# Soft-MoE logits with slots on partitions, one sum of weights per half, and side products placed anew

## The chip, the cores and the metric

The kernel runs on one core of a Trainium2 chip. The metric is the device time of one execution in microseconds (us); less is better. The kernel before takes 743.97 us (median of 3 runs, 743.84 to 745.63). Engines are named as the profile names them: PE is the matrix engine and PEld its weight loads, DVE the vector engine, ACT the scalar engine, POOL the GpSimd engine, SP the engine that issues the DMAs.

## The reference, cut to what matters

Attention over 4 batches of 8 heads (1152 keys, 64 wide, queries pooled in twos to 576) gives x. A soft mixture of experts with 32 slots takes x, and a gated layer follows.

```python
attn = exp(scores - max);  attn = attn / (sum(attn) + 1e-09);  x = attn @ v      # [2304, 512]
logits = x @ phi                                                                 # [2304, 32]
d = softmax(logits, over tokens);  slot_input = d.T @ x                          # [32, 512]
slot_out[e] = relu(slot_input[e] @ w1[e]) @ w2[e]                                # 8 experts
c = softmax(logits, over slots);  x = c @ slot_out
xn = x / rms(x) * rms_g
out = (silu(xn @ w_gate) * (xn @ w_val)) @ w_out
```

## The kernel before

The attention works through 16 pairs of heads, p = 0 to 15, four pairs to a batch. Within a pair the two heads are s = 0, 1; queries lie in two halves h of 288, keys in nine tiles kt of 128. For each (kt, h) `qk` makes scores on PE (line 407, both heads side by side in the array), ACT makes exponentials `e` (L409), POOL adds them up in `acc` (L424), and PE multiplies them with v (`av`, L430). `acc` comes in two parts j for each half: tiles 0 to 4 and 5 to 8. In pairs 0 and 15 the halves come one after the other, and DVE makes part of the sums.

Work is written out by hand in program order, and every engine runs its own instructions in that order. A tile kt is a step; every third (kt = 2, 5, 8) is a visit, in which PE runs, after the scores, three items of the row maximum of a later pair (m1, m2, m3, L350 or L356, each reduced on DVE, L351 or L357, 128 x 1024 numbers) and the products `av` of three tiles (called a, b, c). The table `AT` puts side work at a time in units of kt: 2.75 is late in the first visit, ahead of b, 2.88 ahead of c. `side(p)` collects for pair p the side work of the pair before, l = p - 1: `take_x` copies av out of PSUM (L440), `sums` (2.75) adds the rows of `acc` over the 128 keys with a matmul against ones (L450: two heads, two halves, two parts, each 32 columns wide, so four can stand side by side in the array), `recips` (2.87) turns the sums so that tokens lie on partitions (L459) and takes their reciprocals, `x_logits` (5.78) multiplies x with phi, tokens on partitions (L500), `x_share` and `logit_add` divide and add up over heads (L509, L519, L520), `x_turn` and `x_divide` (8.75) put the finished x with tokens on partitions (L482, L491). At batch ends come `d_turn` and `d_exp` (8.73, 8.85: logits with slots on partitions, L537, and their exponentials, L557, with the add of their sums, L559), `d_back` (2.88, L565), `slot_part` (5.76, L580), `slot_turn` (8.74, L603) and the softmax over slots, `c_soft` (3.5, 5.53, 8.96; L611 to L624). Other side work on DVE: `low_q` (3.2, L308), `low_k` (L314), `turn_64` (0.5, 1.0, 3.3; L714), all with two inputs in SBUF. The two `max_tail` items (L360, L363) stand at 2.85 and 2.86.

All scores, maximum items and side products of PE take their PSUM from one tag of three buffers, in turn:

```python
def two_banks(name):
    return ps.tile([128, 2, 512], F32, tag="u", bufs=3, name=name)
```

so the third tile after a given one takes its buffer, and PE waits until that one has been read. After pair 15 the experts (L975, L998) and the gated layer (L1158, L1206) follow; the weights of the experts come in by DMA as the buffers of the attention come free.

Of the kernel before, what the change touches and what calls it, by code (L numbers as in the profile page):

```python
# [7 lines left out]
F32 = mybir.dt.float32  # L8
# [6 lines left out]
ALU = mybir.AluOpType  # L15
# [46 lines left out]
    x_share=5.785,  # L62
    logit_add=5.79,
# [10 lines left out]
    c_soft=[3.5, 5.53, 8.96],  # L74
# [20 lines left out]
)  # L95
AT_15 = dict(
    take_x=0.24,
    sums=0.8,
    recips=1.33,
    x_turn=[2.3, 3.3],  # L100
    x_divide=[2.4, 3.6],
    x_logits=4.2,
    x_share=4.8,
    drop_x=4.25,
    logit_add=5.22,
# [6 lines left out]
    logit_add_a=6.51,  # L112
# [37 lines left out]
def attention_softmoe_gated_kernel(ctx: ExitStack, tc: tile.TileContext, kT, qT, vv, ip, cst, w1, w2, wg, wv, wo, rg, out):  # L150
# [103 lines left out]
    ipt = one.tile([128, 4, 64], F32, name="ipt")  # L254
    rgt = one.tile([128, 4], F32, name="rgt")
# [185 lines left out]

    def sums(p, hs=(0, 1)):

        n = len(hs)
        o = bank([64 * n, HQ], "sums")
        for j in range(2):
            for s in (1, 0):
                for i, h in reversed(list(enumerate(hs))):
                    g = 32 * (n * s + i)
                    pe.matmul(o[g:g + 32, :], lhsT=ones, rhs=acc[p, h, j][:, s], start=(j == 0), stop=(j == 1))  # L450
        rel("B", 2 * n)
        srow[p] = B([64 * n, HQ], F32, "srow")
        ac.copy(srow[p], o)

    def recips(p, hs=(0, 1)):
        n = len(hs)
        o = bank([TB, 3, 64 * n], "sumt")
        for t in range(3):
            pe.transpose(out=o[:, t, :], in_=srow[p][:, TB * t:TB * t + TB], identity=ident[0:64 * n, 0:64 * n])  # L459
        rel("B")  # L460
        if p not in rr:
            rr[p] = S([TB, 2, 3, 2], "rr")
        r = rr[p][:, hs[0]:hs[-1] + 1]
        dv.tensor_scalar_add(out=r.rearrange("p h t s -> p s h t"),
                             in0=o.rearrange("p t (s h x) -> p s h t x", s=2, h=n)[:, :, :, :, 0], scalar1=1e-9)
        dv.reciprocal(r, r)

    xo, ls = {}, {}
# [59 lines left out]
    def d_turn(g):  # L528
# [80 lines left out]
    def c_max(b):  # L609
        mx = S([TB, NBK], "cmx")  # L610
        dv.reduce_max(out=mx, in_=lg[b], axis=AX.X)  # L611
        t = ct[b] = S([TB, NBK, 32], "ct", bufs=1)
        dv.tensor_tensor(out=t, in0=lg[b], in1=mx[:, :, None].to_broadcast([TB, NBK, 32]), op=ALU.subtract)
# [109 lines left out]
    def side(p):  # L723
# [3 lines left out]
        def at(name, g):  # L727
            ts = (AT_0 if p == 0 else AT_15 if p == NP - 1 else AT).get(name, AT.get(name))
# [22 lines left out]
        if l >= 0:  # L751
            at("take_x", lambda i: take_x(l))
            at("sums", lambda i: sums(l))
# [4 lines left out]
            at("x_logits", lambda i: x_logits(l, range(6)))  # L758
            at("x_share", lambda i: x_share(l, range(6)))
# [25 lines left out]
        if p == NP - 1:  # L785
# [5 lines left out]
            at("x_logits_a", lambda i: (x_logits(p, range(3)), x_share(p, range(3))))  # L791
            at("logit_add_a", lambda i: logit_add(p, (0,)))
# [7 lines left out]
    with tc.manual_schedule():  # L800
# [45 lines left out]
        dv.tensor_copy(identr, ident[0:TB, 0:TB])  # L846

# [455 lines left out]
```

## Time and profile before

| | |
|---|---|
| median of 3 runs | 743.97 us |
| the profiled execution | 744.83 us, of which the span of the page is 742.8 us |
| PE | busy 710.6 us, 96% of the span |
| DVE, ACT, POOL | busy 426.6, 391.7 and 423.3 us |
| pair 8 of the attention | 249.0 to 278.3 us |

The page gives busy times by engine, the span in 40 slices, the DMA queues, the chain of waits that ended last, and the costliest groups of instructions. One fp32 matmul of the program appears as two records (two passes), a transpose as one. A row's busy time merges instructions that follow closely; the start of the next row on the same engine tells when the array was free.

### The profile page before, as it was taken

What the parts mean: (1) busy time and instruction counts of PE and PEld (TensorE: products, weight loads), DVE (VectorE), ACT (ScalarE), POOL (GpSimd) and SP (SyncE); (2) the same over time, 40 slices, a digit from 0 to 9 for tenths busy, and PEclk for the clock granted to TensorE, in tenths of its full rate; (3) what the DMA queues carried; (4) which work ended last, traced back from release to release, by engine and by line L of the source; (5) the groups of instructions that cost most, each with busy time, mean ns of one, the idle gap of its engine ahead of it and who ended that gap; (6) DMA issues with size and microseconds to landing.
All of it is one profiled execution on the core that took longest, in us unless ns stands there. A gap on an engine that the chain in (4) does not pass through costs nothing.

```text
span 742.8 us, 15502 instructions
## 1 busy us (share of the span) xinstructions
PE 710.6 (96%) x6143; PEld 500.3 (67%) x6143; DVE 426.6 (57%) x663; ACT 391.7 (53%) x809; POOL 423.3 (57%) x340
## 2 busy tenths in 40 slices
PE   4999999999999999999999999979999999999998
PEld 2666677675676676676676665544357888888887
DVE  5958666676687675677765763351053755544420
ACT  2455665664665656656655534432155856554320
POOL 5336887866877876678876665320016854535330
PEclk9999999999999999999999999989999999999999
DMA  5222552753635635517514316079991010000001
GB/s 173 96 90 77 184 192 73 254 183 126 237 124 202 238 103 179 206 61 254 182 44 181 129 48 230 6 276 357 374 384 52 15 43 30 29 28 15 29 28 43
DMA packets 52855, 103.57 MB, mean 139 GB/s; under 512 B 5816, under 2 KB 19632, under 8 KB 52784
## 3 DMA queue, kind: packets, MB, share of 16 engines
q1 hardware_dynamic: 52784, 102.59, 39.3%
q8 instruction: 48, 0.79, 0.4%
q14 instruction: 23, 0.19, 0.1%
HBM read 89.39 MB, written 13.11 MB: 138 GB/s over the span
## 4 chain that ended last, share of the span: by engine, by line
PE 88%; DVE 5%; DMA 3%; issue 2%; ACT 1%; POOL 1%; SPq 0%; ACTq 0%; DVEq 0%
PE sc L407 21%; PE av L430 20%; PE yo L1206 20%; PE mxp L350 5%; PE gv L1158 3%; PE sums L450 2%; PE xl L500 2%; PE hin L975 2%; DVE mx L351 2%; PE xo L482 1%; PE so L998 1%; DMA w<-away 1%; PE mxp L360 1%; PE pp L580 1%; DMA w<-in_w_dram 1%
## 5 line engine op out<-in xcount | busy, mean ns | idle before, releaser
L424 POOL TENSOR_TENSOR acc<-acc,e 128x576 f32<-128x576 f32 x148 | 213.9, 1475 | 63.4 <-ACT e L409 57.9
L409 ACT ACTIVATE e<-sc 128x576 f32<-128x576 f32 x288 | 165.7, 658 | 95.4 <-PE sc L407 93.6
L351 DVE TENSOR_REDUCE mx<-mxp 128x2 f32<-128x1024 f32 x120 | 144.3, 1223 | 110.2 <-PE mxp L350 110.1
L430 PE MATMUL av<-e,vt 128*64 128x288 f32 x1152 | 164.7, 416 | 0.0
L424 POOL TENSOR_TENSOR acc<-e 128x576 f32<-128x576 f32 x60 | 84.7, 1432 | 89.6 <-ACT e L409 89.6
L430 PEld LDWEIGHTS av<-e,vt 128*64 128x64 f32 x1152 | 72.6, 136 | 60.1 <-issue 24.1
L1206 PE MATMUL yo<-woh,hA 128*128 128x512 f32 (+1 forms) x312 | 98.9, 384 | 0.0
L407 PE MATMUL sc<-qh,kh 64*128 64x288 f32 x576 | 96.7, 327 | 0.8 <-DVE mx L351 0.6
L407 PE MATMUL sc<-mr,pick 64*128 64x288 f32 x576 | 87.7, 295 | 1.5 <-DMA mr<-mrow 1.5
L407 PE MATMUL sc<-ql,kh 64*128 64x288 f32 x576 | 87.2, 294 | 0.0
L407 PE MATMUL sc<-qh,kl 64*128 64x288 f32 x576 | 87.1, 294 | 0.0
L1163 DVE SCALAR_TENSOR_TENSOR th<-th,gv 128x384 f32<-128x384 f32 x72 | 39.9, 554 | 62.4 <-ACT th L1160 61.8
L1189 POOL TENSOR_TENSOR hA<-hu,hA 128x384 fp32r<-128x384 f32 x48 | 48.9, 1019 | 42.5 <-ACT hA L1188 38.8
L407 PEld LDWEIGHTS sc<-qh,kh 64*128 64x128 f32 x576 | 55.5, 186 | 24.2 <-issue 9.8
L1206 PEld LDWEIGHTS yo<-woh,hA 128*128 128x128 f32 x312 | 57.6, 188 | 10.2 <-issue 0.7
L407 PEld LDWEIGHTS sc<-mr,pick 64*128 64x128 f32 x576 | 56.5, 187 | 1.9 <-DMA mr<-mrow 1.9
L1206 PE MATMUL yo<-wol,hA 128*128 128x512 f32 (+1 forms) x151 | 57.8, 383 | 0.0
L1160 ACT ACTIVATE th<-gv 128x384 f32<-128x384 f32 x72 | 35.2, 490 | 42.4 <-PE gv L1158 38.9
L407 PEld LDWEIGHTS sc<-qh,kl 64*128 64x128 f32 x576 | 56.6, 189 | 0.2
L407 PEld LDWEIGHTS sc<-ql,kh 64*128 64x128 f32 x576 | 56.2, 187 | 0.0
L350 PE MATMUL mxp<-kh,qh 64*128 64x512 f32 x240 | 48.6, 435 | 0.0
L1165 DVE SCALAR_TENSOR_TENSOR hu<-th,gv 128x384 f32<-128x384 f32 x72 | 39.9, 554 | 8.4 <-DVE th L1163 0.5
(192 smaller groups left out, 1040.4 us busy)
## 6 DMA issues: line engine op xcount, KB each, us to landing
w<-in_w_dram SPq DMA_DIRECT2D x86, 256.0 KB
w<-in_w_dram SPq DMA_DIRECT2D x21, 512.0 KB
vt<-in_vv_dram SPq DMA_DIRECT2D x16, 576.0 KB
qraw<-in_qT_dram SPq DMA_DIRECT2D x15, 576.0 KB
kraw<-in_kT_dram SPq DMA_DIRECT2D x15, 576.0 KB
away<-w SPq DMA_DIRECT2D x32, 256.0 KB
w<-away SPq DMA_DIRECT2D x32, 256.0 KB
raw<-in_wg_dram SPq DMA_DIRECT2D x12, 512.0 KB
```

What stands on the lines that cost most here:

```text
L350: pe.matmul(o[:, s, :], lhsT=q[r, 128 * t:128 * t + 128], rhs=k[r, 512 * c:512 * c + 512], start=True, stop=True)
L351: dv.reduce_max(out=heads[:, :, t, c], in_=o, axis=AX.X)
L407: pe.matmul(o[:, s, 0:HQ], lhsT=w[r, wk], rhs=q[r, c], start=(i == 0), stop=(i == 3))
L409: ac.activation(ets[p, kt, h], o[:, :, 0:HQ], AF.Exp, scale=0.0625)
L424: eng.tensor_tensor(out=acc[p, h, j], in0=first[p, h, j] if n == 1 else acc[p, h, j], in1=e, op=ALU.add)
L430: pe.matmul(avt[p, h][64 * s:64 * s + 64, 0:HQ], lhsT=vt[p][:, kt, 64 * s:64 * s + 64], rhs=ets[p, kt, h][:, s], start=(kt == 0), stop=(kt ...
L1158: pe.matmul(o[i], lhsT=sg[n][:, 256 * i + 128 * c:256 * i + 128 * c + 128], rhs=cT[g], start=True, stop=True)
L1160: ac.activation(t, o[0], AF.Tanh, scale=0.5)
L1163: dv.scalar_tensor_tensor(out=t, in0=t, scalar=1.0, in1=o[0], op0=ALU.add, op1=ALU.mult)
L1165: dv.scalar_tensor_tensor(out=u, in0=t, scalar=0.5, in1=o[1], op0=ALU.mult, op1=ALU.mult)
L1189: gp.tensor_tensor(out=b, in0=u, in1=f(a), op=ALU.subtract)
L1206: pe.matmul(o, lhsT=x, rhs=w[:, c], start=(ft == 0 and i == 0), stop=(ft == NF - 1 and i == 2))
```

## The change

The sums of weights: after the pair, DVE adds part 1 of `acc` to part 0 for each half (`sum_up`), and `sums` runs over one part, into rows 64h + 32s. ACT's copy adds 1e-9. The logits: phi is now the stationary side and x the moving one, so slots lie on partitions and 288 tokens stream; the reciprocals of the sums are taken in that layout (`inverse`, two instructions of 128 x 144 in place on `srow`), and `logit_add` multiplies and adds 128 x 288 numbers. The reciprocals for `x_divide` stay. The softmax over slots now needs the logits with tokens on partitions, which `c_turn` makes on PE, and `d_turn` needs a matmul that adds the two heads. Pair 15 keeps the old layout (`x_logits_last`: for each half three matmuls of the old form and one product with the reciprocals), and its logits join in `d_turn` and `c_turn` as further matmuls. In `slot_part`, the last two of six tiles of tokens go in two halves of 256 columns, so that they spread over all four column groups of the array. `recips` loses its addition of 1e-9 (L464). The reduction and the subtraction behind `c_turn` read PSUM in place of SBUF.

```diff
 AT = dict(
...
+    sum_up=[0.1, 0.2],
     sums=2.75,
+    d_back=2.76,
+    d_copy=2.77,
     max_tail=[2.85, 2.86],
     recips=2.87,
-    d_back=2.88,
-    d_copy=2.89,
+    c_turn=2.88,
+    inverse=[3.4, 4.0],
...
     x_logits=5.78,
-    x_share=5.785,
-    logit_add=5.79,
+    logit_add=5.785,
...
-    c_soft=[3.5, 5.53, 8.96],
+    c_soft=[5.53, 8.96],
...
+AT_01 = dict(
+    x_turn=8.85,
+    x_divide=[8.86, 8.87],
+    drop_x=8.88,
+    d_exp=8.84,
+)
 AT_15 = dict(
     take_x=0.24,
+    sum_up=[0.25, 0.26],
     sums=0.8,
     recips=1.33,
+    inverse=[1.4, 2.41],
...
-    x_share=4.8,
     drop_x=4.25,
-    logit_add=5.22,
+    logit_add=4.8,
...
+    def sum_up(p, h):
+        dv.tensor_tensor(out=acc[p, h, 0], in0=acc[p, h, 0], in1=acc.pop((p, h, 1)), op=ALU.add)
+        rel("B")
+
     def sums(p, hs=(0, 1)):
...
+        n = 1 + ((p, hs[0], 1) in acc)
...
+        for j in range(n):
             for s in (1, 0):
...
+                for h in reversed(hs):
+                    g = 64 * h + 32 * s
+                    pe.matmul(o[g:g + 32, :], lhsT=ones, rhs=acc[p, h, j][:, s], start=(j == 0), stop=(j == n - 1))
...
+        ac.activation(srow[p][r], o[r], AF.Copy, bias=1e-9)
...
+    def inverse(p, i):
+        c = slice(HQ // 2 * i, HQ // 2 * i + HQ // 2)
+        dv.reciprocal(srow[p][:, c], srow[p][:, c])
...
+    def x_logits(p):
+
+        o = xl[p] = bank([128, HQ], "xl")
+        for h in range(2):
+            pe.matmul(o[64 * h:64 * h + 64, :], lhsT=ipt[:, p % 4, :], rhs=xu[p][:, HQ * h:HQ * h + HQ], start=True, stop=True)
...
+    def logit_add(p):
         b, hp = divmod(p, 4)
...
+        x, o = srow[p], xl.pop(p)
         if hp:
...
+            dv.tensor_tensor(out=x, in0=o, in1=x, op=ALU.mult)
+            dv.tensor_tensor(out=lg[b], in0=lg[b], in1=x, op=ALU.add)
         else:
...
+            lg[b] = S([128, HQ], "lg")
+            dv.tensor_tensor(out=lg[b], in0=o, in1=x, op=ALU.mult)
+        rel("B")
...
     def d_turn(g):
...
-            for t in range(3):
-                pe.transpose(out=o[i][:, TB * t:TB * t + TB], in_=lg[b][:, 3 * h + t, :], identity=ident[0:TB, 0:TB])
+            r = slice(64 * h, 64 * h + 64)
+            pe.matmul(o[i], lhsT=stack[r, 0:32], rhs=lg[b][r], start=True, stop=(b < 3))
+            for t in range(3 if b == 3 else 0):
+                for s in range(2):
+                    pe.matmul(o[i][:, TB * t:TB * t + TB], lhsT=xl["ls"][:, t, s, h], rhs=ident[0:TB, 0:TB], start=False, stop=(s == 1 and t == 2))
...
     def slot_part(g):
...
+        last = n - 4 if n > 4 else 0
         for j in reversed(range(n)):
...
+            for i in range(2 if j < last else 1):
+                q, c = (32 * (j + 2 * i), slice(256 * i, 256 * i + 256)) if j < last else (32 * (j % 4), slice(0, 512))
+                pe.matmul(o[q:q + 32, c], lhsT=dnx[g][:, j, :], rhs=x[:, c], start=(j >= last), stop=(j < last or not last))
...
-    def c_max(b):
+    def c_turn(b):
+        o = bank([TB, 3, 64], "lgt")
+        for t in range(3):
+            pe.matmul(o[:, t], lhsT=lg[b][:, TB * t:TB * t + TB], rhs=pair.rearrange("p h l -> p (h l)"), start=True, stop=(b < 3))
+            for s in range(2 if b == 3 else 0):
+                pe.matmul(o[:, t], lhsT=ident[0:TB, 0:TB], rhs=xl["ls"][:, t, s].rearrange("p h l -> p (h l)"), start=False, stop=(s == 1))
...
         def at(name, g):
-            ts = (AT_0 if p == 0 else AT_15 if p == NP - 1 else AT).get(name, AT.get(name))
+            ts = (AT_0 if p == 0 else AT_15 if p == NP - 1 else AT_01 if p > 1 and p % 4 < 2 else AT).get(name, AT.get(name))
...
             if p % 4 == 2 and p > 2:
                 b = p // 4 - 1
-                at("c_soft", lambda i: (c_max, c_exp, c_soft2)[i](b))
+                at("c_turn", lambda i: c_turn(b))
+                at("c_soft", lambda i: (c_exp, c_soft2)[i](b))
...
-        c_max(3)
+        c_turn(3)
```

Of the buffers: `srow` is now held until `logit_add`, `sum_up` gives back one part of `acc` earlier, a small tile (`ad`) moves into the slots of tag B, and a tile of the experts moves from the tag of `ls`, which is gone, to that of `lg`.

## Rows read from the trace of the kernel before

**Rows 1.** The page: busy by engine; in slices, granted clock and DMA

```profile
PE 710.6 (96%) x6143; PEld 500.3 (67%) x6143; DVE 426.6 (57%) x663; ACT 391.7 (53%) x809; POOL 423.3 (57%) x340
...
PEclk9999999999999999999999999989999999999999
DMA  5222552753635635517514316079991010000001
```

**Rows 2.** Two stretches: busy by engine (instructions), granted clock, DMA share, GB/s

```profile
249.00:278.30 29.30, 28.81 (x295) 19.89 (x291) 20.40 (x31) 16.93 (x34) 23.93 (x17) 1.00 0.51 176
...
487.00:560.00 73.00, 65.93 (x652) 32.63 (x653) 22.68 (x61) 24.85 (x63) 11.45 (x16) 0.95 0.96 345
```

**Rows 3.** PE timeline, pairs 8 and 9: start us, us, instruction, xrecords, [idle before <-releaser]

```profile
265.32 1.23 PE L500 MATMUL xl<-ipt,xu 128*96 128x64 f32 x12
266.48 2.16 PE L430 MATMUL av<-e,vt 128*64 128x288 f32 x16
...
276.22 2.16 PE L430 MATMUL av<-e,vt 128*64 128x288 f32 x16
...
283.79 1.18 PE L450 MATMUL sums<-acc,ones 128*32 128x288 f32 x16
284.90 1.19 PE L430 MATMUL av<-e,vt 128*64 128x288 f32 x8
```

**Rows 4.** PE in order of time, work at a batch end, pairs 8 and 9

```profile
274.27 0.67 PE L537 MATMUL lgt<-cs,lg 96*32 96x96 f32 x6
275.43 0.86 PE L482 MATMUL xo<-cs,xu 128*96 128x128 f32 x6 [0.49 <-DVE mx L351]
...
288.07 0.47 PE L565 MATMUL dn<-cs,dtx 32*96 32x32 f32 x6 [0.93 <-DVE mx L361]
...
295.20 1.91 PE L580 MATMUL pp<-xt,dn 96*32 96x512 f32 x12
...
307.16 0.86 PE L482 MATMUL xo<-cs,xu 128*96 128x128 f32 x6 [0.50 <-DVE mx L351]
```

**Rows 5.** DVE in order of time, pairs 8 and 9

```profile
263.49 1.23 DVE L351 TENSOR_REDUCE mx<-mxp 128x2 f32<-128x1024 f32 x1 [2.22 <-PE mxp L350]
...
277.44 1.00 DVE L491 TENSOR_TENSOR xt<-xo,rr 96x384 f32<-96x384 f32 x2
278.72 0.15 DVE L559 TENSOR_TENSOR sall<-sm 32x1 f32<-32x1 f32 x1 [0.28 <-ACT dtx L557]
...
283.67 2.36 DVE L351 TENSOR_REDUCE mx<-mxp 128x2 f32<-128x1024 f32 x2 [0.33 <-PE mxp L350]
```

**Rows 6.** DVE by line and shape: busy us, mean ns of one, idle before

```profile
L424 DVE TENSOR_TENSOR acc<-acc,e 128x576 f32<-128x576 f32 x12 | 9.4, 787 | 12.9 <-ACT e L409 6.5 <-POOL acc L424 6.4
...
L519 DVE TENSOR_TENSOR lg<-lg,ls 96x192 f32<-96x192 f32 x11 | 3.9, 354 | 0.4
...
L466 DVE RECIPROCAL rr<-rr 96x12 f32<-96x12 f32 x15 | 3.4, 224 | 0.5
...
L466 DVE RECIPROCAL rr<-rr 96x6 f32<-96x6 f32 x2 | 0.4, 186 | 0.1
```

**Rows 7.** DVE in order of time, starts of pairs 8 and 15

```profile
250.03 1.28 DVE L714 SCALAR_TENSOR_TENSOR w<-w,raw 128x512 uint32<-128x512 uint32 x2
253.64 1.23 DVE L351 TENSOR_REDUCE mx<-mxp 128x2 f32<-128x1024 f32 x1 [2.33 <-PE mxp L350]
...
450.99 0.19 DVE L623 RECIPROCAL csm<-csm 96x6 f32<-96x6 f32 x1
451.21 1.31 DVE L624 TENSOR_TENSOR cn<-ct,csm 96x192 f32<-96x192 f32 x1
```

**Rows 8.** POOL in order of time, the same two stretches

```profile
247.24 5.36 POOL L424 TENSOR_TENSOR acc<-acc,e 128x576 f32<-128x576 f32 x3
...
448.16 5.63 POOL L424 TENSOR_TENSOR acc<-acc,e 128x576 f32<-128x576 f32 x4
```

**Rows 9.** PE in order of time, pair 15

```profile
453.85 0.69 PE L450 MATMUL sums<-acc,ones 128*32 128x288 f32 x8 [0.67 <-POOL acc L424]
```

More of the change, by code (lines that the diff above doesn't have):

```diff
@@ L111 @@
     x_logits_a=6.15,
-    logit_add_a=6.51,
     d_exp_a=7.18,
@@ L254, in attention_softmoe_gated_kernel @@
     ipt = one.tile([128, 4, 64], F32, name="ipt")
+    pair = one.tile([128, 2, 32], F32, name="pair")
     rgt = one.tile([128, 4], F32, name="rgt")
@@ L440, in take_x @@
             ac.copy(xu[p][:, HQ * h:HQ * h + HQ], avt.pop((p, h))[:, 0:HQ])
+    def sum_up(p, h):
+        dv.tensor_tensor(out=acc[p, h, 0], in0=acc[p, h, 0], in1=acc.pop((p, h, 1)), op=ALU.add)
+        rel("B")
     def sums(p, hs=(0, 1)):
-        n = len(hs)
-        o = bank([64 * n, HQ], "sums")
-        for j in range(2):
+        n = 1 + ((p, hs[0], 1) in acc)
+        r = slice(64 * hs[0], 64 * hs[-1] + 64)
+        o = bank([128, HQ], "sums")
+        for j in range(n):
             for s in (1, 0):
[L448 to L453, printed above, removed]
+                for h in reversed(hs):
+                    g = 64 * h + 32 * s
+                    pe.matmul(o[g:g + 32, :], lhsT=ones, rhs=acc[p, h, j][:, s], start=(j == 0), stop=(j == n - 1))
+        rel("B", n * len(hs))
+        srow[p] = B([128, HQ], F32, "srow")
+        ac.activation(srow[p][r], o[r], AF.Copy, bias=1e-9)
     def recips(p, hs=(0, 1)):
         n = len(hs)
+        q = slice(64 * hs[0], 64 * hs[-1] + 64)
         o = bank([TB, 3, 64 * n], "sumt")
         for t in range(3):
-            pe.transpose(out=o[:, t, :], in_=srow[p][:, TB * t:TB * t + TB], identity=ident[0:64 * n, 0:64 * n])
-        rel("B")
+            pe.transpose(out=o[:, t, :], in_=srow[p][q, TB * t:TB * t + TB], identity=ident[q, q])
+        if p == NP - 1:
+            rel("B")
         if p not in rr:
             rr[p] = S([TB, 2, 3, 2], "rr")
[L463 to L468, printed above, removed]
+        dv.reciprocal(rr[p][:, hs[0]:hs[-1] + 1], o.rearrange("p t (h s x) -> p h t s x", s=2, h=n)[:, :, :, :, 0])
+    def inverse(p, i):
+        c = slice(HQ // 2 * i, HQ // 2 * i + HQ // 2)
+        dv.reciprocal(srow[p][:, c], srow[p][:, c])
+    xo = {}
     def x_turn(p, js):
@@ L757, in side @@
             at("drop_x", lambda i: rel("B"))
-            at("x_logits", lambda i: x_logits(l, range(6)))
-            at("x_share", lambda i: x_share(l, range(6)))
+            at("inverse", lambda i: inverse(l, i))
+            at("x_logits", lambda i: x_logits(l))
             at("logit_add", lambda i: logit_add(l))
@@ L846, in attention_softmoe_gated_kernel @@
         dv.tensor_copy(identr, ident[0:TB, 0:TB])
+        for h in range(2):
+            r = slice(64 * h, 64 * h + 64)
+            dv.tensor_copy(pair[r, h], stack[r, 0:32])
+            dv.memset(pair[r, 1 - h], 0.0)
         def next_max(p, mx):
@@ L904, in attention_softmoe_gated_kernel @@
         dv.reduce_max(out=gm, in_=mall[:, 0:4], axis=AX.X)
-        o, z = bank([TB, 3, 2, 32], "xo"), bank([TB, 3, 128], "xo")
-        x = [xu[l][:, TB * j:TB * j + TB] for j in (3, 4, 5)]
+        x_logits_last(1)
+        z = bank([TB, 3, 128], "xo")
         for i in range(3):
-            pe.matmul(o[:, i].rearrange("p s l -> p (s l)"), lhsT=x[i], rhs=ipt[:, l % 4, :], start=True, stop=True)
-        for i in range(3):
-            pe.transpose(out=z[:, i, :], in_=x[i], identity=ident)
+            pe.transpose(out=z[:, i, :], in_=xu[l][:, HQ + TB * i:HQ + TB * i + TB], identity=ident)
         rel("B")
         r = rr[l][:, 1]
-        dv.tensor_tensor(out=ls[l][:, 3:6], in0=o, in1=r[:, :, :, None].to_broadcast([TB, 3, 2, 32]), op=ALU.mult)
-        logit_add(l, (1,))
         for i in range(3):
```

48 lines of the change are left out of this document (19 added, 29 removed).

## The prediction

> **What bounds the kernel now.** I read the page first: PE is busy for 96% of the span, DVE, ACT and POOL for little over half, and the granted clock is full in nearly every slice [rows 1]. PE's record times are modelled, so a busy PE proves little; what does is the next view, PE in order of time. There each record starts where the array is free again: the sums step on after 1.11 us, the logits after 1.16, and products, maximum items and scores follow without a hole except where a small wait is printed [rows 3, 4]. In the attention PE's queue sets the pace, and an instruction taken from it is time taken from the kernel, as long as nobody is late next. Two more readings set the limits. In pair 8 DVE is busy for 20.4 and POOL for 23.9 of 29.3 us [rows 2]: little room. And behind the attention, 487 to 560 us, DMA is at 0.96 of its time [rows 2]: expert weights set the pace there. That burst begins when the attention frees its buffers (the slice before it has a DMA share of 0 tenths [rows 1]), so it moves with the end of the attention and gives nothing back by itself.
>
> **Part by part.** The sums: eight matmuls, four column groups, two parts, 1.11 us from row to row [rows 3]. With one part half of them go: 0.55 us. Pairs 1 to 14 do this: 14 x 0.55 = 7.7 us.
>
> The logits: before, twelve records of 64 columns and a 96-column weight load each, 1.16 us from row to row [rows 3]. After, two matmuls of 288 columns in two column halves. That is the form of `av`: eight such records take 1.19 us, less the 0.07 by which a row overlaps the next (265.32 + 1.23 against 266.48), 1.12 us [rows 3]; four are 0.56. The saving is 0.60, in 15 pairs 9.0 us. Gross: 16.7 us.
>
> What DVE gets for it: `sum_up` is two additions of 128x576; their like takes 787 ns on the mean [rows 6], 1.57 us. `inverse` has no like in the trace: two reciprocals of 144 numbers per partition. The nearest rows are 224 ns for 12 and 186 ns for 6 [rows 6]: 6.3 ns a number, so 224 + 132 x 6.3 = 1.06 us each. If the row's time were all per number, 2.7 us; if only 1 ns a number came on top (as 354 ns for 192 numbers allow [rows 6]), 0.36. I take 1.06, since two sizes give a slope. `logit_add` (two of 288 numbers, some 0.45 each by the same slope) replaces 0.54 + 2 x 0.35, the first by the like of `x_divide` [rows 5, 6]: -0.3. In sum +3.2 us a pair on an engine that is idle for some 9 [rows 2].
>
> Where it lies decides. The reciprocals (3.4, 4.0) come before the first maximum item of the second visit, where DVE idles 2.22 us [rows 5]: 2.12 fit, nothing is late. `sum_up` stands at a pair's start. There POOL still adds the last tile: in pair 8 its three additions run from 247.24 to 252.60, stretched by two `turn_64` on DVE (250.03, 1.28 us) [rows 7, 8]. That stretching goes both ways: beside running POOL additions a DVE instruction with two SBUF inputs, 96x192, takes 1.31 us (451.21) in place of 354 ns [rows 6 to 8]. So `sum_up` waits up to one addition (5.63 / 4 = 1.41 us), cannot begin its second part before POOL's last addition is done, and the two `turn_64` are queued behind it, and behind those m1, whose readers are the PSUM buffers. Worked out for pair 8: `x_divide` ends where the next row begins, about 250.1 [rows 7]; POOL's third addition, unstretched, at 247.24 + 3 x 1.41 = 251.5 [rows 8]; `sum_up` at 252.0 and 252.8, the two `turn_64` at 254.1, while m1 can begin at 253.64 [rows 7]: 0.4 late, 0.7 if POOL comes second. In the first visit DVE has 0.33 us to spare [rows 5], and with shorter sums PE comes to the buffer of m3 just as it is freed, so 0.1 to 0.4 us shows on PE. I take 0.3 in the five plain pairs (2, 3, 4, 8, 12), 0.6 in 7 and 11 (the slot softmax is queued there as well), 0.1 in 6, 10, 14: 3.0 us. Bounds: 0 (POOL's stretch hides all) to 1 us in each of 14.
>
> [...]
>
> Batch ends, each three times. Pairs 5, 9, 13: `d_back` waits 0.93 us for a maximum item [rows 4]; moved ahead of b it waits for m2, which DVE ends 1.2 us after it begins (283.67 + 1.2 [rows 5]) while PE is there at 284.35: 0.5, so 0.43 less. `slot_part` has twelve records, 1.91 us less the overlap; one and a half rounds in place of two is 1.4, 0.43 less. The transposes of x wait 0.50 us (307.16) [rows 4]; behind b they find their buffer free. Together -1.35 each, -4.05 us. Pairs 6, 10, 14: `c_turn` is half of twelve logit records, 0.58 us, and stands where `d_back` stood, as third tile after the first tail item, so it inherits a wait of 0.9 [rows 3, 4]: +1.5 each, +4.5. Pairs 4, 8, 12: `lgt` gets no dearer (0.56 against 0.67), the wait of 0.49 for x's transposes goes [rows 4], but `d_exp` now stands ahead of `x_divide`, so the add of its sums, which waits for ACT until 278.72, holds up `x_divide` (1.00 us) until 279.9 [rows 5]. The third score tile of pair 9, PE at some 278.3 + 1.07 (the end of `av`, 276.22 + 2.16 [rows 3], and two tiles of scores), needs that buffer: 0.5 late against before: +0.55 each, +1.65. Batch ends together: +2.1, bounds -4 to +6.
>
> The last pair and the tail. In pair 15 the sums already wait for POOL (0.67 us, then the second half to 454.5) [rows 9]. Now they wait for POOL's end (448.16 + 5.63 [rows 8]) and for one addition of 0.79 [rows 6]: they end about 455.1, +0.7 against before, so `sums` saves nothing here. `d_turn` has for each half of pair 15 twelve records more and two DVE additions (some 0.25 to 0.35 us each) less: +0.5, twice. `c_turn(3)` is 18 records, 1.7 us, in the stage paced by DMA: I take 0.3 of 0 to 1.7. Together +2.0, bounds 0 to 4. Buffers: `srow` is held longer and part of `acc` shorter, no load of weights hangs on it; 0.
>
> The sum against the profiled execution's 744.83 us (742.8 of span): -16.7 + 3.0 + 2.1 + 2.0 = -9.6, 735.2. The median of the runs stands 0.86 lower: 734.4.
>
> **The rivals.** (a) Nobody is late: `sum_up` lies in DVE's idle time and the waits at batch ends cancel. For it: 2.33 us before m1 at the plain pair's start [rows 7] would hold 1.57. Against: POOL's last addition is in just that stretch [rows 8]. Only the tail remains: 744.0 - 16.7 + 2 = 729, or less.
>
> (b) DVE's lock with POOL spreads: slower. Place: the reciprocals at 3.4 and 4.0. If each waited for POOL's running addition (1.41 us), or cost 2.7 us, the pair's DVE work would be 2.6 to 3.1 us late at the second visit. PE comes back to m1's buffer with the logits (265.32 [rows 3]) 0.6 us after it is freed (263.49 + 1.23 [rows 5]), so about 2 us of new waiting in each of 14 pairs, 28 us, stand against the gain of 9.6: 762, and still 749 with half of it hidden. It decides from 9.6 / 14 = 0.7 us of new PE waiting a pair. Against: a reciprocal at 450.99 takes 0.19 us while POOL runs on [rows 7, 8], as the 186 ns alone [rows 6]; so it isn't shut out. It has 6 numbers only, and the size is extrapolated.
>
> [...]
>
> (c) Saved PE time turns into waiting for DVE in every pair: 0.5 to 0.7 us at m3's buffer. For it: m1, m2 and m3 follow each other on DVE with 0.33 us to spare [rows 5], and half a microsecond less on PE uses up what lies behind m3. Against: before the second visit DVE idles 2.22 us [rows 5], and the logits, too, shorten PE behind the maximum items only; so the first of three visits alone is that tight. Result 741 to 745.
>
> (d) The change doesn't do what it says: the two logit matmuls don't run side by side, and take 1.1 us. Then 9 us are missing: 743. Against: `av` has the same column halves and streams.
>
> **How the numbers follow.** My forecast 0.60 (own range 729 to 739), (a) 0.17, (b) 0.08, (c) 0.11, (d) 0.04. The range 727 to 742 leaves out the lower half of (a), half of (c) and (b), some 2 in 10. Within 0.3% (2.2 us, about what a measurement can tell from no change) lie most of (c) and (d). Faster 0.80, same 0.12, slower 0.08.
>
> **What would show it.** Right: `sums` eight records in some 0.6 us, logits four in some 0.6; RECIPROCAL 128x144 near 1.06 us; m1 at plain pairs' starts up to 0.7 us late behind `sum_up`; a wait of 0.9 ahead of `c_turn`; the wait at `d_back` halved; pair 15's sums waiting about 2 us. The expert stage as long as before. Wrong: PE waiting over 0.7 us a pair for DVE, POOL's additions stretched far beyond 1.5 us, or a tail that grows by what the attention saves.

## The result: 1.2% slower, where 1.3% faster was forecast

The kernel after takes 753.61 us (median, 753.19 to 754.5), the kernel before 744.8 us beside it (743.84 to 746.28): ratio 1.0118, interval 1.0096 to 1.014. The forecast was 734.4 us, its range ended at 742. The profiled execution took 753.71 us, of which the span is 751.7, 8.9 more than before. Its page, the line that answers to the first of [rows 1]:

```profile
PE 706.1 (94%) x5967; PEld 490.8 (65%) x5967; DVE 480.7 (64%) x691; ACT 391.4 (52%) x809; POOL 427.5 (57%) x340
```

PE has 4.5 us less to do and the kernel is longer all the same: PE waits more. DVE is busy for 54 us more, 3.9 a pair over 14 pairs, where the forecast gave it 3.2 (its own terms, 1.57 + 2.12 - 0.3, make 3.4). That is a first hint: as the rows of pair 8 below show, a record counts as busy while its instruction waits for POOL (1.9 us for a turn that takes 0.64 without a wait). Two plain pairs that do the same work, 8 and 12, and the stage paced by DMA, by windows (stretch; length, busy of PE, PEld, DVE, ACT, POOL; granted clock, DMA share, GB/s), as [rows 2]:

```profile
255.10:285.85 30.75, 28.53 (x273) 18.89 (x271) 25.05 (x29) 16.22 (x32) 22.49 (x17) 0.94 0.46 161
369.95:399.17 29.22, 26.98 (x273) 18.17 (x271) 25.06 (x29) 16.21 (x32) 22.52 (x17) 1.00 0.38 138
493.00:567.00 74.00, 67.18 (x679) 35.00 (x676) 23.04 (x62) 24.54 (x62) 11.36 (x16) 0.93 0.98 349
```

Pair 8 took 28.5 us before, counted, as all pairs from here on, from its first score record (249.83) to that of pair 9 (278.31). PE stands idle for 2.2 us in each of the two, and pair 8 has a granted clock of 0.94 beside it. The last line is the stage of the expert weights, as full of transfers as before (a DMA share of 0.98, before 0.96 [rows 2]); its 74 us are the length of the stretch chosen here, and by the table below all that the kernel loses from pair 15 on is the 4.0 us of that pair (experiment 7).

By stages, from the starts of each pair's first score record in the two profiled executions, against the forecast's terms:

```
stage              forecast   measured
pair 0                 0        +2.2
pair 1               -1.15      +2.4
pair 2               -0.85      +2.7
pair 3               -0.85      -0.2
pairs 4, 8, 12       -0.3 each  -0.5, +2.3, +0.7
pairs 5, 9, 13       -2.5 each  -1.6, -1.6, -1.6
pairs 6, 10, 14      +0.45 each +0.5, +0.5, +0.5
pairs 7, 11          -0.55 each -0.6, -1.1
pair 15 to the end   +1.4       +4.0
sum                  -9.6       +8.6, and 0.3 ahead of pair 0
```

Pairs 1, 2, 8 and 15 hold most of the difference (12 of 18 us). The start of pair 8, DVE in order of time (start us, us, instruction, xrecords, [idle before <-releaser]), against [rows 7]:

```profile
254.38 1.01 DVE L508 TENSOR_TENSOR xt<-xo,rr 96x384 f32<-96x384 f32 x2
255.37 2.64 DVE L452 TENSOR_TENSOR acc<-acc 128x576 f32<-128x576 f32 x2
257.94 3.73 DVE L743 SCALAR_TENSOR_TENSOR w<-w,raw 128x512 uint32<-128x512 uint32 x2
261.59 3.47 DVE L360 TENSOR_REDUCE mx<-mxp 128x2 f32<-128x1024 f32 x3
```

POOL in the same stretch:

```profile
251.18 5.55 POOL L433 TENSOR_TENSOR acc<-acc,e 128x576 f32<-128x576 f32 x4
257.84 3.28 POOL L433 TENSOR_TENSOR acc<-e 128x576 f32<-128x576 f32 x2 [1.12 <-ACT e L418]
261.08 1.85 POOL L302 TENSOR_TENSOR qs<-qraw 128x576 f32<-128x576 f32 x1
```

And PE there, then in pair 12:

```profile
258.46 0.40 PE L359 MATMUL mxp<-kh,qh 64*128 64x512 f32 x2
...
262.86 0.69 PE L464 MATMUL sums<-acc,ones 128*32 128x288 f32 x8 [2.22 <-DVE mx L360]
263.48 1.56 PE L439 MATMUL av<-e,vt 128*64 128x288 f32 x8
...
377.72 0.69 PE L464 MATMUL sums<-acc,ones 128*32 128x288 f32 x8 [2.23 <-DVE mx L360]
378.35 1.19 PE L439 MATMUL av<-e,vt 128*64 128x288 f32 x8
```

Read them together. `sum_up` (L452) begins while POOL's last addition runs and takes 2.64 us for two instructions whose median is 0.75 (1.97 for the first, which ends 0.62 behind the end of that addition, and 0.74). Then the two `turn_64`, 1.28 us before [rows 7], take 3.73: each starts behind the start of a POOL addition (the two of the row at 257.84) and waits for it: the turns take 1.91 and 1.90 us and end 0.55 behind the ends of the two additions (259.85 and 261.67 against 259.30 and 261.12). PE has m1 ready at 258.86 (258.46 + 0.40), and DVE takes it at 261.59, 2.7 us late. `sums` needs m1's buffer and waits 2.22 us. After the wait in pair 8 the next eight `av` records take 1.56 us in place of 1.19, at a granted clock of 0.72 (263.48 to 265.04). In pair 12 the same wait is followed by 1.19 us at a granted clock of 1.00, and the pair is 1.5 us shorter. The granted clock of the stretch in pair 8, and then of the only one of its kind that the attention of the kernel before has, in pair 1:

```profile
264.20:267.60 3.40, 3.40 (x14) 1.83 (x12) 2.23 (x4) 0.00 (x0) 1.46 (x2) 0.50 0.72 255
...
50.80:54.20 3.40, 3.40 (x30) 3.40 (x28) 1.94 (x2) 1.95 (x3) 0.34 (x1) 0.51 0.83 291
```

The same four DVE instructions in pair 7 of the same execution, and POOL beside them:

```profile
230.47 1.42 DVE L452 TENSOR_TENSOR acc<-acc 128x576 f32<-128x576 f32 x2
231.81 1.28 DVE L743 SCALAR_TENSOR_TENSOR w<-w,raw 128x512 uint32<-128x512 uint32 x2
...
231.10 4.64 POOL L433 TENSOR_TENSOR acc<-e 128x576 f32<-128x576 f32 x2 [1.19 <-ACT e L418]
```

Here they take 2.6 us, from 230.47 to 233.09, and it is POOL that waits: its two additions, 1.4 us each, take 4.64 (3.27 for the first, beside the second addition of `sum_up` and the two turns). The slot softmax on DVE has put `sum_up` off until POOL's last addition is done. So in both pairs one of the two engines is held up beside the other, but which of them waits differs, and PE pays much only where it is DVE (2.22 us at the sums in pair 8, 0.38 in pair 7).

### The profile page after: what moved, and what is told of

Same layout as the page of the kernel before. It is cut to its first block, busy times and chain, and to the rows that moved or that the text cites. A ratio compares the mean times of both kernels' runs of the same rounds, so it can differ in the third digit from the quotient of the medians.

```text
span 751.7 us, 15214 instructions
## 1 busy us (share of the span) xinstructions
PE 706.1 (94%) x5967; PEld 490.8 (65%) x5967; DVE 480.7 (64%) x691; ACT 391.4 (52%) x809; POOL 427.5 (57%) x340
## 4 chain that ended last, share of the span: by engine, by line
PE 76%; DVE 12%; DMA 6%; ACT 2%; issue 2%; SPq 1%; POOL 1%; DVEq 0%; ACTq 0%
PE yo L1237 20%; PE av L439 18%; PE sc L416 17%; DVE mx L360 4%; PE mxp L359 4%; DMA w<-in_w_dram 3%; PE gv L1189 3%; DVE w L743 3%; DVE acc L452 2%; DMA kraw<-in_kT_dram 1%; PE xl L516 1%; PE mxp L369 1%; PE sums L464 1%; DMA w<-away 1%; PE hin L1006 1%
## 5 line engine op out<-in xcount | busy, mean ns | idle before, releaser
L433 POOL TENSOR_TENSOR acc<-acc,e 128x576 f32<-128x576 f32 x148 | 208.8, 1440 | 70.6 <-ACT e L418 61.2
L439 PE MATMUL av<-e,vt 128*64 128x288 f32 x1152 | 170.5, 426 | 0.0
L433 POOL TENSOR_TENSOR acc<-e 128x576 f32<-128x576 f32 x60 | 92.9, 1568 | 86.5 <-ACT e L418 86.5
L439 PEld LDWEIGHTS av<-e,vt 128*64 128x64 f32 x1152 | 75.4, 140 | 64.2 <-issue 28.5
```

Of the source, the lines that this page charges most:

```text
L433: eng.tensor_tensor(out=acc[p, h, j], in0=first[p, h, j] if n == 1 else acc[p, h, j], in1=e, op=ALU.add)
L439: pe.matmul(avt[p, h][64 * s:64 * s + 64, 0:HQ], lhsT=vt[p][:, kt, 64 * s:64 * s + 64], rhs=ets[p, kt, h][:, s], start=(kt == 0), stop=(kt ...
```

## The experiments

Each was run beside the kernel before on the same chip; the ratios are against that one. A diff is against the kernel after, unless it says otherwise.

**1. Without `sum_up`.**

```diff
-            at("sum_up", lambda i: sum_up(l, i))
```

> The changed kernel with the DVE additions taken out: PE sums both parts of the weights again, all else stays changed. Theory (DVE and POOL exclude each other at a pair's start, m1 comes late, PE waits at the sums, and a stretch of half clock follows a long wait): the waits at the sums go in pairs 2, 3, 4, 7, 8, 12 (8.9 us) and shrink by 3.3 us in pair 15, the half-clock stretches in pairs 2, 8 and 15 go (1.7 us each), PE gets 15 x 0.55 = 8.3 us back: 753.6 - 12.2 - 5.1 + 8.3 = 744.6, 739 to 746. Rival (the reciprocals and the new logits layout make DVE late): the waits stay, 753.6 + 8.3 = 762.

740.33 us against 745.71, ratio 0.993 (0.9915 to 0.9944): faster than both. Pair 8, DVE and then PE:

```profile
249.55 1.28 DVE L743 SCALAR_TENSOR_TENSOR w<-w,raw 128x512 uint32<-128x512 uint32 x2
253.16 1.23 DVE L360 TENSOR_REDUCE mx<-mxp 128x2 f32<-128x1024 f32 x1 [2.33 <-PE mxp L359]
```

```profile
254.83 1.18 PE L464 MATMUL sums<-acc,ones 128*32 128x288 f32 x16
```

One line gone, and the two turns are back at 1.28 us, DVE waits for m1 instead of m1 for DVE, and no plain pair has any idle time of PE. So the reciprocals and the new logits, which are still in, cost these pairs nothing.

**2. `sum_up` alone**, on the kernel before (the other parts left out).

```diff
+    sum_up=[0.1, 0.2],
...
+            at("sum_up", lambda i: sum_up(l, i))
```

> The kernel before with only the DVE additions and the sums over one part; logits, batch ends and layouts as before. Theory: the same waits as in the changed kernel, 12 us at the sums and some half-clock stretches behind them, against 14 x 0.55 = 7.7 us less on PE: 750 to 755. Rival (reciprocals and layout): 744.8 - 7.7 = 737.

757.81 us, ratio 1.017 (1.0153 to 1.0187): above the range of the theory, though the profiled execution, the fastest of the four, took 753.39. The waits at the sums of the kernel after come back to within 0.05 us in pairs 2, 3, 4, 7, 8 and 15; in pair 12 it is 0.92 in place of 2.23. Pair 8:

```profile
261.22 0.69 PE L457 MATMUL sums<-acc,ones 128*32 128x288 f32 x8 [2.22 <-DVE mx L353]
```

Nothing else of the change is needed for the loss: `sum_up` alone costs more than the whole change, and the other parts, with their own wait in pair 1 (experiment 8), take some of it back. The wait of pair 8 is followed by no slow stretch here (granted clock 1.00 over the pair).

**3. One part for all nine tiles.** POOL adds all tiles into one part, so there is nothing to add up on DVE.

```diff
-PART = 5
+PART = 9
...
-            at("sum_up", lambda i: sum_up(l, i))
```

> The changed kernel without a second part at all: POOL adds all nine tiles of a half into one sum, two additions of 1.41 us more per pair on POOL, none on DVE, and PE sums one part. Theory: no DVE addition waits for POOL and m1 is on time, but POOL has 26.7 of 27 us and its additions end 2.8 us later after a pair; sums wait for POOL instead where that is over some 5 us after the start: 738 to 750. Rival (DVE late for another reason): the waits for DVE at the sums stay, 753.

745.06 us, ratio 0.9996 (0.9979 to 1.0013): no change against before. The waits at the sums are gone in plain pairs, and others appear: 0.7 us for a maximum item at the transposes of x or the logits in pairs 3, 4, 7, 8 and 12, 1.4 us for x in 5, 9 and 13, and 2.4 us for POOL in pair 15. That PE takes one-part sums without a wait when DVE has no `sum_up` agrees with the theory; how the longer chain of POOL's additions makes the new waits was not followed.

**4. The turns behind the sums.**

```diff
-    turn_64=[0.5, 1.0, 3.3],
+    turn_64=[2.95, 2.96, 3.3],
```

> The kernel after with the two turn_64 of a pair's start placed behind the sums (2.95 and 2.96 in place of 0.5 and 1.0); sum_up stays at 0.1 and 0.2. Theory (sum_up and the two turns wait one after the other for POOL's running additions, and m1 stands behind all of them): with the turns gone sum_up alone ends at about m1's time, the sums wait 0 to 0.5 us for DVE in pairs 2, 8 and 12 (2.2 in the kernel after) and in 3 and 4 (0.9), and the half-clock stretches behind the long waits go; the turns may cost up to 1 us a pair behind m3. Time 743 to 748 us against 753.6. Pair 15's wait of 4.0 us stays. Rival 1 (the two additions of sum_up alone are enough to make m1 late): waits of over 1 us stay, 750 to 754. Rival 2 (the reciprocals or the new logits cost the time): no change, 753 to 754.

750.54 us, ratio 1.0064 (1.0041 to 1.0087); 3 us less than the kernel after, and just above the range of the theory. Pair 8, DVE and then PE:

```profile
250.82 2.64 DVE L452 TENSOR_TENSOR acc<-acc 128x576 f32<-128x576 f32 x2
254.37 1.23 DVE L360 TENSOR_REDUCE mx<-mxp 128x2 f32<-128x1024 f32 x1 [0.91 <-PE mxp L359]
...
261.98 1.91 DVE L743 SCALAR_TENSOR_TENSOR w<-w,raw 128x512 uint32<-128x512 uint32 x1
```

```profile
256.04 0.69 PE L464 MATMUL sums<-acc,ones 128*32 128x288 f32 x8
```

`sum_up` is as stretched as before (2.64), but alone it fits: DVE is 0.91 us early for m1 and the sums wait for nobody. So rival 1 falls: it takes `sum_up` and the turns behind it together. The two turns now stand ahead of `low_q` and the third turn, which meets POOL's next additions (1.91 us); behind it the logits wait 1.27 us for a maximum item in the plain pairs (3.14 in pair 7). Most of the wait moved to the second visit.

**5 and 6. Idle work in place of the wait.** PE runs matmuls of constants into unused columns of the `av` accumulator ahead of the sums.

```diff
+    def fill(p):
...
+        for i in range(FILL.get(p, 0)):
+            for s in (1, 0):
+                pe.matmul(avt[p, 0][64 * s:64 * s + 64, 288:480], lhsT=cs[:, 64 * s:64 * s + 64], rhs=cs[:, 0:192], ...)
...
+            at("sums", lambda i: fill(p))
```

> The kernel after with idle work on PE ahead of the sums: matmuls of 192 columns into unused columns of the accumulator, 0.19 us a pair of them as an estimate, 11 pairs in pairs 2, 8 and 12, 4 in 3 and 4, 1 in 7, 19 in pair 15, about as long as PE waits for DVE there. Nothing that the output needs is changed. Theory (the waits are followed by a half-clock stretch, which costs some 1.7 us more each): the sums begin no earlier, but the stretches in pairs 2, 8 and 15 are gone and those pairs are 1.5 to 2 us shorter each: 747 to 750 against 753.6, though PE does more work. Rival (the waits alone cost, the clock falls for another reason): the stretches stay, 753 to 756.

756.14 us, ratio 1.015 (1.0124 to 1.0175). The size was wrong by two: a pair of these matmuls is four records and takes 0.38 us (44 records in 3.80; the 0.19 is what two records of 192 columns come to where eight of 288 take 1.12 [rows 3]), so 11 pairs filled more than the wait. Still, pairs 8 and 12, 1.5 us apart in the kernel after, became alike (30.65 us), both at a granted clock of 1.00. Then sized by that trace:

> The kernel after with idle work on PE ahead of the sums, as in the run before it of that kind, but sized by its trace: there a pair of the 192-column matmuls took 0.38 us (4 pairs 1.52), so 11 of them were 4.2 us where PE had waited 2.2, and pairs 12 and 8 grew alike to 30.65 us. Now 5 pairs in pairs 2, 8 and 12 (1.9 us), 2 in 3 and 4 (0.8), 9 in pair 15 (3.4). Nothing that the output needs is changed. Theory (a long wait of PE can be followed by a half-clock stretch, which costs 1.5 us more: pair 8 with one took 30.74, pair 12 with the same wait and none 29.22): pair 8 falls to pair 12's time, pair 2 by as much, the stretch in pair 15 goes: 747 to 751 against 753.6. Rival (the stretches don't come from the waits): they stay, 753 to 755.

747.57 us, ratio 1.003 (1.0013 to 1.0047): 6 us less than the kernel after by the medians, with more work on PE. The profiled execution is the slowest of ten (751.12 us) and 2.6 us shorter than that of the kernel after: pairs 2 and 8 are 1.5 us shorter each, pair 3 is 1.3 longer. Windows of pairs 8 and 12, then PE in pair 8:

```profile
254.54:283.80 29.26, 28.79 (x291) 19.43 (x289) 25.06 (x29) 16.10 (x32) 22.50 (x17) 1.00 0.48 170
367.88:397.17 29.29, 28.83 (x293) 19.43 (x291) 25.07 (x29) 16.10 (x32) 22.53 (x17) 1.00 0.38 142
```

```profile
260.00 1.85 PE L459 MATMUL av<-cs 128*64 128x192 f32 x20
262.32 0.69 PE L474 MATMUL sums<-acc,ones 128*32 128x288 f32 x8 [0.47 <-DVE mx L360]
262.94 1.19 PE L439 MATMUL av<-e,vt 128*64 128x288 f32 x8
```

The sums of pair 8 begin as late as before (7.78 us into the pair, 7.76 in the kernel after), but `av` behind them runs at 1.19 and the pair is 1.5 us shorter. With PE kept busy through the wait the slow stretch does not follow, in pairs 2 and 15 either, with both sizes of the fill (granted clock 1.00; over the whole profiled execution 0.993 and 0.991, in the kernel after 0.984). In kernels without the fill pair 2 has the stretch behind this wait in all three (after, experiments 2 and 7; 0.984, 0.984 and 0.986 over the whole execution), pair 8 in two of them. So in these runs the price behind the wait hangs on PE standing still.

**7. The last pair without `sum_up`.**

```diff
-            at("sum_up", lambda i: sum_up(l, i))
+            if p < NP - 1:
+                at("sum_up", lambda i: sum_up(l, i))
```

> The kernel after without sum_up in the last pair alone: there PE sums both parts as before. Theory (sum_up waits for POOL's end in pair 15, PE waits 4.0 us for it, and a half-clock stretch follows): the wait falls to 0.7 us, the sums are 0.55 longer, the stretch goes, the pair begins its expert work 4 to 5 us earlier and the whole is 749 to 750 against 753.6. Rival (the stage behind it is paced by transfers that started before, so the wait in pair 15 is hidden): 752.5 to 754.

748.59 us, ratio 1.0033 (1.0012 to 1.0054). From pair 15 to the end it takes 291.63 us in place of 295.56. In the kernel after the row of DVE's second addition and PE's row there are

```profile
459.42 1.94 DVE L452 TENSOR_TENSOR acc<-acc 128x576 f32<-128x576 f32 x1 [1.29 <-POOL acc L433]
```

```profile
461.50 0.69 PE L464 MATMUL sums<-acc,ones 128*32 128x288 f32 x8 [3.99 <-DVE acc L452]
```

and in this kernel

```profile
455.14 0.69 PE L464 MATMUL sums<-acc,ones 128*32 128x288 f32 x8 [0.67 <-POOL acc L433]
```

The rival, that a stage paced by transfers hides the wait, falls: 4 us in pair 15 are 4 us at the end.

**8. Two placements more**, on the kernel of experiment 1.

```diff
-    c_turn=2.88,
+    c_turn=2.76,
...
-            at("inverse", lambda i: inverse(l, i))
+            if p == 1:
+                todo += [(5.76, len(todo) + i, lambda i=i: inverse(l, i)) for i in range(2)]
+            else:
+                at("inverse", lambda i: inverse(l, i))
```

> The kernel after without sum_up (as the first experiment) and two placements more: c_turn ahead of the tail maxima (2.76 for 2.88), and in pair 1 the two reciprocals behind the last maximum (5.76, 5.77 for 3.4, 4.0). Theory: c_turn waits 0.5 in place of 0.93 us in pairs 6, 10 and 14 (-1.3 together); in pair 1 the logits' wait of 2.1 us goes and the row of maxima is ready earlier, so the wait of 1.5 us for it in pair 2 falls as well (-2 to -3.5). 735 to 737.5 against 740.3 for the first experiment. Rival (DVE has c_turn's maximum and subtraction ahead of the tail's maxima, and the wait moves there; pair 1's saving returns at the scores): 739 to 741.

735.94 us, ratio 0.9881 (0.9857 to 0.9906). The waits at `c_turn` went altogether (0.93 to 0, not 0.5). In pair 1 of the kernel after DVE and PE had

```profile
66.25 1.46 DVE L317 TENSOR_TENSOR ql<-qs,qh 128x576 fp32r<-128x576 f32 x1
67.64 1.90 DVE L743 SCALAR_TENSOR_TENSOR w<-w,raw 128x512 uint32<-128x512 uint32 x1
69.47 1.95 DVE L483 RECIPROCAL srow<-srow 128x144 f32<-128x144 f32 x2
```

```profile
72.55 0.81 PE L516 MATMUL xl<-xu,ipt 128*64 128x288 f32 x4 [2.12 <-DVE mx L360]
73.13 3.75 PE L439 MATMUL av<-e,vt 128*64 128x288 f32 x16
```

and with the reciprocals behind the last maximum item the logits wait 0.31:

```profile
69.40 0.71 PE L516 MATMUL xl<-xu,ipt 128*64 128x288 f32 x4 [0.31 <-DVE mx L360]
```

The wait for the row of maxima (1.5 us, a DMA) did not fall, and 0.74 us of the gain came back at the scores.

**9. `d_exp` behind `x_divide`**, on experiment 8's kernel.

```diff
-    d_exp=8.84,
+    d_exp=8.875,
```

> The fastest kernel so far with one placement changed: in pairs 4, 5, 8, 9, 12 and 13 d_exp behind x_divide (8.875 for 8.84). Theory (the addition of d_exp's sums waits for ACT and x_divide stands behind it on DVE; that is the 0.41 us for which the third score tile of pairs 5, 9 and 13 waits): these waits go, -1.2 us, 734.5 to 735 against 735.9. Rival (the wait moves to d_back or to the next maximum item): no change.

733.13 us, ratio 0.9829 (0.9814 to 0.9844). The 0.41 us of pairs 5, 9 and 13 are gone, and they are 0.6 us shorter each (30.16 to 29.5): a little more than expected. This is the fastest version with a plain schedule, 1.7% under the kernel before.

**10. `sum_up` at another place**, on experiment 8's kernel. The first reciprocal here overwrites half of the sums before `recips` has turned them, so x is scaled otherwise; the instructions are the same in number and size.

```diff
+            if p < NP - 1:
+                at("sum_up", lambda i: sum_up(l, i))
...
-    sums=2.75,
+    sum_up=[2.95, 2.96],
+    sums=4.5,
...
-    recips=2.87,
+    recips=5.4,
-    inverse=[3.4, 4.0],
+    inverse=[4.9, 5.76],
-    low_q=3.2,
+    low_q=7.25,
```

> The fastest kernel so far with sum_up again, placed behind the tail maxima (2.95, 2.96), where POOL idles for 1.9 us in that kernel's pair 8, outside the last pair; behind it move the sums (4.5), recips (5.4), one reciprocal (4.9) and the other behind the last maximum (5.76), and low_q goes to 7.25, where DVE idles 2.1 us. Theory (sum_up cost time by its place beside POOL's additions, not by its work): the sums take 0.62 in place of 1.18 us, nobody waits over 0.3 us for DVE, 13 x 0.55 = 7 us less than the 735.9 of the same kernel without it, less 1 to 3 for the queue: 730 to 732. Rival (DVE has no 1.5 us left anywhere in a pair that PE doesn't pay for): waits for DVE of 0.5 to 1 us in each pair, 736 or more.

768.42 us, ratio 1.0304 (1.0286 to 1.0322): the rival, and by more than it said. DVE and then PE in and ahead of pair 8's second visit:

```profile
271.80 3.20 DVE L452 TENSOR_TENSOR acc<-acc 128x576 f32<-128x576 f32 x2
```

```profile
275.15 0.69 PE L464 MATMUL sums<-acc,ones 128*32 128x288 f32 x8 [1.47 <-DVE acc L452]
```

`sum_up` takes 3.2 us: in this kernel POOL idles for only 0.47 us there (before 272.97), and DVE meets its additions again. In the third visit of the pair before, where `low_q` now stands, it takes 1.98 us beside POOL (at 256.79), and PE waits 1.63 us for a maximum item. So this run refutes the place and not the theory that the place decides.

**11 and 12. `sum_up` only where no wait was seen**, on experiment 9's kernel: in pairs 5, 6, 9, 10, 11, 13 and 14, and in 5, 9, 11 and 13.

```diff
+            if p in (5, 6, 9, 10, 11, 13, 14):
+                at("sum_up", lambda i: sum_up(l, i))
```

> The fastest kernel so far with sum_up back at its place (0.1, 0.2), but only in the seven pairs in which the kernel after showed no wait of PE for DVE at the sums: 5, 6, 9, 10, 11, 13, 14. Theory (what decides is whether DVE's queue at the pair's start meets POOL's additions, pair by pair): the sums are 0.55 us shorter in seven pairs and nobody waits, 733.1 - 3.9 = 729.3, 728.5 to 731. Rival (in those pairs, too, sum_up costs what it saves, and it was hidden behind other waits there, the 0.47 at d_back and the 0.93 at c_turn, which the fastest kernel no longer has): 732.5 to 735.

> The same with sum_up in pairs 5, 9, 11 and 13 alone. Theory: 733.1 - 2.2 = 730.9, 730 to 732. Rival: 732.5 to 734.5; if the seven lose and these four gain, the wait sits in 6, 10 and 14.

732.73 us (0.9794 to 0.9869 of before) and 732.68 us (0.9799 to 0.985): the same as experiment 9 within what can be told. The first interval reaches from 730 to 736 us, so the pairs have to decide. Pairs 5 and 11 of experiment 9, by windows:

```profile
162.42:191.95 29.53, 29.53 (x302) 19.52 (x301) 20.53 (x28) 18.82 (x40) 20.70 (x16) 1.00 0.50 171
330.23:356.87 26.64, 26.64 (x275) 18.34 (x273) 21.08 (x29) 17.30 (x34) 20.77 (x16) 1.00 0.54 190
```

the same two with the seven, and PE in its pairs 5 and 6:

```profile
161.11:190.64 29.53, 29.06 (x294) 19.25 (x292) 21.87 (x30) 18.94 (x40) 21.00 (x16) 1.00 0.47 158
...
328.90:355.05 26.15, 26.15 (x267) 18.07 (x266) 23.32 (x31) 17.33 (x34) 22.94 (x16) 1.00 0.55 189
```

```profile
168.01 0.47 PE L585 MATMUL dn<-cs,dtx 32*96 32x32 f32 x6 [0.47 <-DVE mx L360]
...
197.27 0.72 PE L634 MATMUL lgt<-pair,lg 128*96 128x64 f32 x6 [0.47 <-DVE mx L360]
```

Pair 5 keeps its 29.53 us to the hundredth: PE is busy 0.47 us less and waits 0.47 us more. The sums are shorter, the maximum item whose buffer comes next is no earlier, and the saved time is handed over to that wait. Of the seven pairs only pair 11 gains, 0.5 us; PE waits for nobody there. The rival was right in the other six.

## Why the prediction was wrong

**The step that failed** is the queue behind `sum_up`: "the two `turn_64` at 254.1, while m1 can begin at 253.64 [rows 7]: 0.4 late, 0.7 if POOL comes second", and with it 0.3 us of PE in plain pairs and bounds of 0 to 1 us. The runs showed 2.2 us in pairs 2, 8 and 12, 0.9 in 3 and 4, 0.4 in 7 and none in 11. The ground was read rightly: POOL's last addition is in that stretch, and DVE and POOL hold each other up there (three additions of POOL take 5.36 us, against 1.41 each in the row of pair 15) [rows 7, 8]. `sum_up` itself was sized rightly too: forecast to end 2.7 us behind `x_divide` (250.1 to 252.8), it takes 2.64, with one wait for POOL. What was wrong is the price of the two turns behind it, 1.28 us, which the forecast ran back to back. They took 3.73, since POOL's next tile had come by then and each turn waited for one of its additions, and m1 was 2.7 us late in place of 0.4. In all, three of the four DVE instructions wait for one POOL addition each (1.97, 1.91 and 1.90 us): 2.8 us of work (two of 0.75, two of 0.64) take 6.2 (255.37 to 261.59).

The trace of the kernel before had both prices. The 1.28 us in pair 8 [rows 7] are two turns that ran while POOL waited for them. In its pair 1 `low_q` and one turn run while POOL adds, and the turn alone takes 1.91:

```profile
64.14 1.46 DVE L308 TENSOR_TENSOR ql<-qs,qh 128x576 fp32r<-128x576 f32 x1
65.52 1.91 DVE L714 SCALAR_TENSOR_TENSOR w<-w,raw 128x512 uint32<-128x512 uint32 x1
```

A duration was carried to another place without asking what runs beside it there, and which of the two would wait. In pairs 7 and 11 the forecast took 0.6 us, for the slot softmax queued ahead; there the same queue kept `sum_up` out of the way of POOL's last addition.

What in the two engines makes one wait for the other no run shows; the traces show the times, 1.9 us for a turn beside a POOL addition and 0.64 without a wait.

**What was not foreseen at all** is the price behind a wait. Pairs 8 and 12 differ by 1.5 us at the same wait and the same work, and pair 8 has the granted clock of 0.94. Pairs 1, 2, 8 and 15 of the profiled execution have such a stretch (in pair 1 the sixteen `av` records take 3.75 us, elsewhere 2.16 [rows 3]; in pair 15 two score records behind the wait take 0.45, elsewhere 0.30); the granted clock is 0.56 over 73.13 to 76.88 us, 0.52 over 93.96 to 97.02, 0.50 over 264.2 to 267.6 and 0.61 over 462.12 to 466.55. The kernel before has one in pair 1 as well, so three are new; at 1.5 us each, an estimate from pairs 8 and 12, that is 4.5 of the 18.5 us between forecast and result. The fills of experiments 5 and 6 show that it hangs on PE standing still; which wait is followed by one is not shown, as pair 12 was spared, and so was pair 8 of experiment 2 at the same 2.22 us.

**Pair 1** is a second failed step: the reciprocals come "where DVE idles 2.22 us [rows 5]: 2.12 fit, nothing is late". That was read in pair 8. It holds in pairs 2 to 14, where experiment 1 has no wait at the logits. In pair 1 `low_q` and the turn ahead of them run beside POOL's additions and take 1.46 and 1.90 us (0.69 and 0.68 in pair 8), as they did before, and with the two reciprocals, 1.95 us, behind them the maximum item is late: 2.1 us of wait. That was the place of the second rival, in one pair of fifteen and by another mechanism; the reciprocals themselves are not held up (1.95 us in pair 1 and in pair 8).

**The last pair**: forecast +0.7 for the sums. POOL ends 0.6 us later than before (3.2 against 2.6 us into the pair), and the second addition, in place of 0.79, takes 1.94: it waits for POOL's end and then for POOL's next addition (459.35). The wait is 3.99 us; experiment 7 takes 4 us out of the pair.

**What held.** The gross: sums 0.62 us a row, logits 0.53 (273.93 to 274.46), and pair 11, where nobody waits, is 1.14 us shorter, as forecast gross (0.55 + 0.60):

```profile
273.93 0.71 PE L516 MATMUL xl<-xu,ipt 128*64 128x288 f32 x4
274.46 2.11 PE L439 MATMUL av<-e,vt 128*64 128x288 f32 x16
```

The batch ends: `d_back` waits 0.47 (forecast 0.5), `c_turn` 0.93 (0.9), `slot_part` takes 1.43 from row to row (302.65 to 304.08; forecast 1.4), and the third score tile of pairs 5, 9 and 13 waits for x:

```profile
287.86 0.40 PE L416 MATMUL sc<-qh,kh 64*128 64x288 f32 x2 [0.40 <-DVE xt L508]
```

That wait was booked to pairs 4, 8 and 12 and shows one pair later, which is half of the 0.9 us that 5, 9 and 13 lack; the other half was not followed. The reciprocal of 144 numbers takes 1015 ns on the mean, forecast 1060:

```profile
L483 DVE RECIPROCAL srow<-srow 128x144 f32<-128x144 f32 x30 | 29.4, 1015 | 0.0
```

From 224 ns for 12 numbers [rows 6] to 1015 for 144 the step is 6.0 ns a number, where the forecast's slope was 6.3.

**The rivals.** (b), slower, was the side on which it came out, with DVE's lock with POOL as its mechanism, but its place, the reciprocals, was refuted by experiments 1 and 2. The first named place, `sum_up` and the turns, had been priced and put into the forecast's own sum: 0.3 us a plain pair, a seventh to a third of the wait that it caused there. (c), saved PE time that turns into waiting, holds in six pairs to two hundredths of a microsecond (experiment 11).

**Pair 0** was 2.2 us longer in the profiled execution, where the change does nothing. Its first products, before and after:

```profile
21.28 1.68 PE L430 MATMUL av<-e,vt 128*64 128x288 f32 x12
...
22.43 3.04 PE L439 MATMUL av<-e,vt 128*64 128x288 f32 x12
```

The same twelve records take nearly twice as long after: score records go from 0.44 us to 0.30 at 20.2 us before and at 25.6 after, some 5 us later. The granted clock is 1.00 in both executions from 16 to 28 us, so this is not the stretch of pair 8, and what it is the traces do not show. Kernels with the same pair 0 took 31.5 (experiment 9) to 33.8 us (experiment 6, the second fill), so it is not the change's.

**Open** are why the records of pair 0 got short later, which waits of PE are followed by a slow stretch, and what decides whether DVE or POOL goes first: in pairs 7 and 8 a POOL addition is recorded as begun up to 0.1 us ahead of a DVE instruction (231.10, 257.84), and in pair 7 POOL waits, in pair 8 DVE.

## What to carry to other kernels

Price an instruction by where it will run, not by where the row stands: here an addition or a turn on DVE cost its 0.64 to 0.75 us beside POOL, or 1.9 to 2.0 where it waited for a POOL addition, and so did each one of its kind queued behind it, down to the one somebody waits for. Both prices were in this trace, 2.6 and 6.2 us for the same four, and only the second cost PE much. Ask of each saving which wait stands next behind it; if another engine ends that wait, and no earlier than before, the saving is handed to it. The good parts of this change (logits 0.6 us a pair, the batch ends) were worth 12 us once `sum_up` was out and three placements were mended.

## What was not expected of the hardware

- Which of DVE and POOL is held up differs from pair to pair: two `sum_up` and two turns, 2.8 us alone, took 6.2 in pair 8, where three of them waited for a POOL addition each, and 2.6 in pair 7, where POOL waited and its two additions took 4.64 us in place of 2.8.
- A reciprocal from SBUF to SBUF of 144 numbers was not held up by POOL: 1.95 us for two, in pair 1 beside running additions as in pair 8, where POOL is idle beside the first.
- A PE wait of 2.2 us cost 3.7 in pair 8, with 1.5 us more in a stretch at a granted clock of 0.50, and 2.2 in pair 12, where the granted clock stayed at 1.00.
- Idle matmuls in the wait made the kernel 6 us faster by the medians than without them (747.57 and 753.61 us), 2.6 us in the profiled executions.
